# First strip of all 576 tokens of batch 0, second of 448, and batch 1's x by token

## The chip, the core and the metric

The kernel runs on one core of one Trainium2 chip. The metric is the device time of one execution in microseconds (us). The kernel before was timed three times: 312.16, 312.21 and 312.97, median 312.21. One further execution was profiled; it took 312.61, of which 310.8 is the span from the program's first to its last instruction.

## What is computed

Linear attention without softmax, a norm per head, and a bilinear feed-forward layer behind it. B=8 batches, H=8 heads, S=576 tokens, D=64; d_model=512, d_ff=1536; 4608 tokens in all.

```python
kv  = einsum('bhsd,bhse->bhde', k, v)
o   = einsum('bhsd,bhde->bhse', q, kv)
x   = o / sqrt(mean(o * o, axis=-1) + 1e-6) * g_norm
x   = x.transpose(0, 2, 1, 3).reshape(B * S, H * D)
out = ((x @ w_a) * (x @ w_b)) @ w_out
```

Inputs and output are fp32 in DRAM; the products run in bf16 and accumulate in fp32.

## The kernel before

**Tiling.** Heads go in pairs (NP=4), so that a pair fills 128 partitions. `xt` holds x with features on partitions and all 4608 tokens along the free side. The feed-forward layer works in 9 strips of 512 tokens (STRIP). A `Unit` is one of 12 blocks of d_ff (fc) of one strip: `part_a` makes four products (one per 128 features, kc) with `wa_t` into a PSUM bank and ScalarE copies it to `a_sb`; `part_b` does the same with `wb_t`, and VectorE multiplies bank and copy into `abt`. `ffn_ab` is one such unit with banks that rotate. After the 12 units the strip's output follows: `ffn_o` makes 12 products per group of 128 tokens, and `o_out` copies the bank to one of four `o_sb` and stores it from the SP queue.

**Two ways to x.** Batches 0 and 1 (EARLY) load q, k and v per pair with the cast to bf16 (`load_pair`). TensorE transposes q (`qtr`), makes kv (`kv1`), then x by feature: `px` for batch 0, `x` for batch 1 (with `kvb`, kv of two heads on the diagonal); ScalarE squares it (`psq`), TensorE sums the squares by a product with `ones` and ScalarE takes the root (`pss`), VectorE multiplies into `xt` (`pst`). Batches 2 to 7 make x by token: `load_late` copies q to a DRAM tile `qs` and loads k and v in another order, `transpose_q` brings q in transposed by a DMA from the SP queue; `tx` makes x of 128 tokens at a time (chunk c, five chunks of which the last has 64 tokens) in 40 small products; `tsq` squares (ScalarE), `tss` sums (VectorE), `trs` takes the root (ScalarE) and multiplies by g (GpSimd), `txt` multiplies (VectorE) and writes the chunk into `xt` by a DMA transpose from the SP queue.

**Order.** The order of every engine is written by hand (`manual_schedule`). The sequence is: batch 0's attention pair by pair; strip 0's units (from u0, line 539); then from line 567 strip 0's output groups, with batch 1's attention between their halves (`pieces`, lines 574 to 591); then strip 1's first two units (592 to 597); then the loop over strips from line 632, in which `slot(A, s, n)` places the by-token steps of batch s+1 between the units: in strip 1 kv of batch 2 stands at n=5 and `tx` at n=6.5. `halves` splits each product into two of 64 stationary columns.

**Queues.** The GpSimd (POOL) queue issues all loads with a cast, in this order: the rest of batch 0, the first 256 columns of wa and wb, the other five blocks of 256 columns, the twelve pieces of wo, batch 1's four pairs, `load_late(2)`. The SP queue issues stores and DMA transposes. Line 570 holds SP's queue until v of batch 1 has landed, before it loads `g_all`.

Of the kernel before, what the change touches and what calls it, by code (L numbers as in the profile page):

```python
# [9 lines left out]
BF16 = mybir.dt.bfloat16  # L10
# [5 lines left out]
def kernel(  # L16
# [26 lines left out]
    EARLY = 2  # L43
    KORD = tuple(range(KC))

    pool = ctx.enter_context(tc.tile_pool(name="sb", bufs=1))
    psum = ctx.enter_context(tc.tile_pool(name="ps", bufs=1, space=bass.MemoryType.PSUM))

    def sb(shape, dt, name):
        return pool.tile(shape, dt, name=name, tag=name)  # L50
# [15 lines left out]

    qT = [sb([128, NP, S], BF16, f"qT{i}") for i in range(2)]
    kvs = [sb([128, NP, D], BF16, f"kvs{i}") for i in range(2)]

    kvb = sb([128, NP, 128], BF16, "kvb")  # L70
    xt = sb([128, KC, n_tok], BF16, "xt")
    abt = [[sb([128, STRIP], BF16, f"ab{i}_{f}") for f in range(FC)] for i in range(2)]
    a_sb = [sb([128, STRIP], BF16, f"asb{i}") for i in range(4)]
    sq = [sb([128, 2, HF], BF16, f"sq{i}") for i in range(3)]
    rs = [sb([128, 2, HF], FP32, f"rs{i}") for i in range(3)]
# [53 lines left out]
    def load_ab(c0, c1):  # L129
        nc.gpsimd.dma_start(out=wa_t[:, :, c0:c1], in_=wa_v[:, :, c0:c1])  # L130
        nc.gpsimd.dma_start(out=wb_t[:, :, c0:c1], in_=wb_v[:, :, c0:c1])
# [27 lines left out]
    def product(o, lhsT, rhs, **kw):  # L159
        for r in (slice(0, D), slice(D, 2 * D)) if halves[0] else (slice(0, 2 * D),):  # L160
            nc.tensor.matmul(o[r], lhsT=lhsT[:, r], rhs=rhs, **kw)  # L161


    class Attn:
# [18 lines left out]
                        stop=(c == len(rows) - 1),  # L183
                    )

        def kv_out(self, ps, src):
            for j in range(2):
                r = slice(j * D, (j + 1) * D)
                nc.scalar.copy(kvb[r, ps, r], src[r])


        def kv1(self, p, i):
            self.kv(p, P[:, i, STRIP - D :])
# [56 lines left out]
                )  # L250


        def x(self, p, i0):
            for h in range(2):
                product(
                    P[:, i0 + h, 0:HF],
                    kvb[:, p, :],
                    self.qT[:, p, h * HF : (h + 1) * HF],
                    start=True,
                    stop=True,  # L260
                )

        def rows(self, c):
            t0 = min(c * 128, S - 128)
# [19 lines left out]
        def tx(self, lent):  # L286
            self.lent = lent
            for c in range(LC + 1):
                t0, _ = self.rows(c)
                for p in range(NP):  # L290
                    for j, (i, c0) in enumerate(self.place(c)):
                        r = slice(j * D, (j + 1) * D)
                        nc.tensor.matmul(  # L293
                            P[:, i, c0 + p * D : c0 + (p + 1) * D],
                            lhsT=self.qT[r, p, t0 : t0 + 128],
                            rhs=self.kvs[r, p, :],
                            start=True,
                            stop=True,
                        )


            _, r = self.rows(LC)
            for j, (i, _) in enumerate(self.place(LC)):
                nc.scalar.copy(
                    x_last[r, j], P[r, i, 0 : STRIP // 2].rearrange("t (p d) -> t p d", p=NP)
                )

        def tsq(self, c):
            _, r = self.rows(c)
# [7 lines left out]
                axis=mybir.AxisListType.X,  # L317
            )

        def trs(self, c):  # L320
            _, r = self.rows(c)
            n = r.stop - r.start
            nc.scalar.activation(  # L323
                rst[c % 3][r],
                sst[c % 3][r],
                AF.Abs_reciprocal_sqrt,
                bias=eps_t[r],
                scale=1.0 / D,
            )
            nc.gpsimd.tensor_mul(  # L330
                sqt[c % 3][r].rearrange("t j p d -> t (j p) d"),
                rst[c % 3][r].unsqueeze(2).to_broadcast([n, H, D]),
                g_all[r].unsqueeze(1).to_broadcast([n, H, D]),
            )
# [13 lines left out]
    class Unit:  # L348
        n = 0

        def __init__(self, s, fc, a, b):
            self.s, self.fc, self.a, self.b = s, fc, P[:, a, :], P[:, b, :]
            self.t = a_sb[Unit.n % 4]
            Unit.n += 1

        def mm(self, w, kcs):
            t0 = self.s * STRIP
            for kc in kcs:
                product(
                    self.a if w is wa_t else self.b,  # L360
                    w[:, kc, self.fc * 128 : (self.fc + 1) * 128],
                    xt[:, kc, t0 : t0 + STRIP],
                    start=(kc == KORD[0]),
                    stop=(kc == KORD[-1]),
                )
# [2 lines left out]
            self.mm(wa_t, kcs)  # L368
            self.mm(wb_t, kcs)

        def part_a(self, kcs=KORD):
            self.mm(wa_t, kcs)
            nc.scalar.copy(self.t, self.a)  # L373

        def part_b(self, kcs=KORD):
            self.mm(wb_t, kcs)
            nc.vector.tensor_mul(abt[self.s % 2][self.fc], self.b, self.t)  # L377

        def rest(self, kcs=KORD):
            self.part_a(kcs)  # L380
            self.part_b(kcs)

    ab_banks = [4, 1, 2, 0]

    def ab_bank():
        ab_banks.append(ab_banks.pop(0))
        return ab_banks[-1]

    def ffn_ab(s, fc, between=None):
        u = Unit(s, fc, ab_bank(), 0)  # L390
        u.part_a()
        if between:
            between()
        u.b = P[:, ab_bank(), :]
        u.part_b()

    def store(t0, t, e0, e1, eng=nc.sync):
# [14 lines left out]
    n_o = [0]  # L412

    def o_mm(s, g, i, fcs, e0=0, e1=d_model):
        for fc in fcs:
            product(
                P[:, i, e0:e1],
                abt[s % 2][fc][:, g * 128 : (g + 1) * 128],
                wo_t[:, fc, e0:e1],
                start=(fc == 0),  # L420
                stop=(fc == FC - 1),
            )
# [41 lines left out]
    make_identity(nc, ident, nomemset=True)  # L464
    nc.scalar.activation(warm, eps_t, AF.Abs_reciprocal_sqrt)
    nc.vector.memset(ones, 0.0)
    nc.vector.memset(kvb, 0.0)
    for t in ktl + vtl:
        nc.vector.memset(t[S - 128 * LC :, :, LC, :], 0.0)
    nc.vector.memset(ones[0:D, 0:D], 1.0 / D)  # L470
# [4 lines left out]
    for c in range(0, KC, 2):  # L475
        for w, src in ((wa_t, wa_v), (wb_t, wb_v)):
            nc.gpsimd.dma_start(out=w[:, c : c + 2, 0:WC], in_=src[:, c : c + 2, 0:WC])  # L477
    for i in range(1, d_ff // WC):
        load_ab(i * WC, (i + 1) * WC)
    for i in range(FC):  # L480
        load_o(i)
    for p in range(NP):
        load_pair(1, p)
    load_late(2)

    X, SS = (4, 0), 6

# [65 lines left out]
    u1.part_a((3,))  # L553
    u0.part_b((2, 3))
    u1.part_b((2, 3))

    u2 = Unit(0, 2, 0, 1)
    u3 = Unit(0, 3, 2, 0)
# [1 line left out]
    u3.part_a()  # L560
    u2.part_b()
    u3.part_b()
    for fc in range(4, FC):
        ffn_ab(0, fc)


    A = Attn(1)
    h1, h2 = range(0, FC // 2), range(FC // 2, FC)

    nc.sync.dma_start(out=gate_d, in_=vt[1][0:1, H - 1, EC - 1, D - 1 : D])  # L570
    nc.sync.dma_start(out=g_all, in_=g_norm.partition_broadcast(128))
    transpose_q(2)
    ffn_o(0, 0, X[0])
    pieces = [(1, h1), (1, h2), (2, h1), (2, h2), (3, h1), (3, h2)]
    for n, (g, fcs) in enumerate(pieces):

        halves[0] = n > 0
        o_mm(0, g, O, fcs)
        if fcs is h2:
            o_out(0, g, O)  # L580
        if 0 <= n - 2 < NP:
            A.pss(n - 2, SS)
            A.pst(n - 2, X[n % 2])
        if 0 <= n - 1 < NP:
            A.x(n - 1, X[(n - 1) % 2])
            A.psq(n - 1, X[(n - 1) % 2])
        if n < NP:
            A.qtr(n, 2)
            A.kv1(n, 2)
            A.kv_out(n, P[:, 2, STRIP - D :])  # L590
            A.qtr_out(n, 2)
    u0 = Unit(1, 0, 2, 3)
    u1 = Unit(1, 1, 4, 5)
    u0.first((0, 1, 2))
    u1.first((0, 1, 2))
    u0.rest((3,))
    u1.rest((3,))
    ab_banks[:] = [0, 1, 2]


    def slot(A, s, n):

        kb = P[:, 7, :].rearrange("q (b p e) -> q b p e", b=2, e=D)
        if s == 1:
            k0, xs = 5, (6.5, 8, 9.5, 11, 12.5)
        else:
            k0, x0 = {2: (2, 3.5), 3: (4, 5.5), 4: (0, 1.5), 5: (4, 5.5), 6: (0, 1.5)}[s]
            xs = tuple(x0 + x for x in (0, 1.5, 2.5, 4, 5))

        k0, x0 = {1: (5, 6.5), 2: (1, 2.5), 3: (4, 5.5), 4: (0, 0.5), 5: (4, 5.5), 6: (0, 0.5)}[s]  # L610
        if n == k0 and s in (1, 2, 3, 5):
            halves[0] = s < 5
            two = [A] if s < 3 else [A, Attn(s + 2)]
            for i, a in enumerate(two):
                for p in range(NP):
                    a.kv(p, kb[:, i, p, :])
            for i, a in enumerate(two):
                (nc.scalar.copy if i else nc.vector.tensor_copy)(a.kvs, kb[:, i])  # L618
        m = n - x0
        if m == 0:  # L620
            A.tx(ab_bank())
        for c in range(LC + 1):
            if m == 1.5 * c:
                A.tsq(c)
            if m == (1, 2, 4, 5, 7)[c]:
                A.tss(c)
            if m == (1, 2, 4, 5, 7)[c] + 0.5:
                A.trs(c)
            if m == (1, 2, 4, 5, 7)[c] + 1.5:
                A.txt(c)  # L630

    for s in range(1, N_STRIP - 1):
# [64 lines left out]
```

## Time and profile before

| What | Value |
|---|---|
| median of three runs | 312.21 us |
| profiled execution | 312.61 us |
| its span | 310.8 us |
| first feed-forward product | 14.10 us |
| strip 0's units end, first output group starts | 35.15 us |
| third unit of strip 1 starts | 53.41 us |
| strip 2 starts | 82.75 us |
| last weight block (wb) landed | 29.40 us |
| last load of batch 1 landed | 46.22 us |
| load_late(2): first issue, last landing | 41.34, 60.65 us |
| load_late(3): first issue, last landing | 62.39, 78.89 us |

The times of the lower rows are counted from the span's start and come from the timeline and from the issues with their landings. In lines of the profile, PE is TensorE, PEld its weight loads, DVE VectorE, ACT ScalarE, POOL GpSimd, SP the sync engine; `L161` is line 161 of the kernel. A form such as 128*64 128x512 is a product with 128 rows and 64 stationary columns that writes 512 columns. Lines of digits give the busy share of 40 equal slices of the span in tenths. "q0 software_dynamic" is the queue of DMAs issued by POOL, q1 that of SP; "share of 16 engines" can exceed 100% because packets overlap.

### The profile page before, as it was taken

The page shows a single profiled execution, that of the slowest core. Times are in us where ns is not written, and L with a number is a line of the kernel's source. Part 1 is how long each engine was busy: PE and PEld are TensorE (multiplying, and loading weights), DVE is VectorE, ACT ScalarE, POOL GpSimd, SP SyncE. Part 2 cuts the span into 40 slices and gives each one's busy share as a digit, 9 for nine tenths or more (in the row PEclk, how much of TensorE's full clock was granted, in tenths as well). Part 3 has the DMA queues.
Part 4 walks back from the last instruction along what each step waited for, and adds up shares of the span by engine and source line. Part 5 has one row for each costly group of instructions (what it writes and reads, how often), then busy time and mean ns, then how long its engine had stood idle before and what let it go on. Part 6 is the DMA issues. An engine that isn't in the chain of part 4 may idle for free.

```text
span 310.8 us, 6542 instructions
## 1 busy us (share of the span) xinstructions
PE 304.3 (98%) x2684; PEld 157.6 (51%) x2701; DVE 140.6 (45%) x235; ACT 117.0 (38%) x231; POOL 101.3 (33%) x123
## 2 busy tenths in 40 slices
PE   7899999999999999999999999999999999999996
PEld 3444476655555555555555555444444444444444
DVE  4544335458248603484386123752782143214321
ACT  3743255354255313551564034632651233123310
POOL 8954991093274630043646300221240000000000
PEclk9999999999999999999999999999999999999999
DMA  8999999999899999047998990073021200030002
GB/s 180 197 196 199 201 188 168 161 169 184 174 137 185 139 174 193 2 84 134 178 177 118 162 188 2 19 160 110 20 51 42 103 1 0 34 103 0 0 36 101
DMA packets 94403, 36.29 MB, mean 117 GB/s; under 512 B 64934, under 2 KB 89894, under 8 KB 94374
## 3 DMA queue, kind: packets, MB, share of 16 engines
q0 software_dynamic: 59120, 18.44, 56.6%
q1 hardware_dynamic: 34786, 16.93, 25.0%
q10 hardware_dynamic: 468, 0.51, 0.6%
q8 instruction: 21, 0.34, 0.5%
q14 instruction: 8, 0.07, 0.1%
HBM read 37.78 MB, written 12.98 MB: 163 GB/s over the span
## 4 chain that ended last, share of the span: by engine, by line
PE 79%; DMA 12%; POOL 7%; issue 1%; ACT 0%; POOLq 0%
PE P L161 77%; DMA wb_t<-in_moe_w_b_dram 6%; DMA vtl<-in_v_dram 4%; DMA wo_t<-in_moe_w_out_dram 2%; PE P L293 1%; PE P L178 1%; POOL vt L119 1%; POOL qt L119 1%; POOL qs L142 1%; POOL kt L119 1%; POOL wa_t L477 0%; POOL wb_t L477 0%; POOL wo_t L134 0%; POOL ktl L145 0%; POOL vtl L145 0%
## 5 line engine op out<-in xcount | busy, mean ns | idle before, releaser
L377 DVE TENSOR_TENSOR ab<-P,asb 128x512 bf16<-128x512 f32 x108 | 74.4, 691 | 103.2 <-PE P L161 99.9
L161 PE MATMUL P<-xt,wb_t 128*64 128x512 bf16 (+1 forms) x641 | 111.4, 379 | 0.2
L161 PE MATMUL P<-xt,wa_t 128*64 128x512 bf16 (+1 forms) x636 | 111.0, 379 | 0.6 <-issue 0.2
L373 ACT CAST asb<-P 128x512 bf16<-128x512 f32 x108 | 63.1, 586 | 89.6 <-PE P L161 89.5
L161 PE MATMUL P<-wo_t,ab 128*64 128x512 bf16 (+3 forms) x673 | 95.5, 371 | 0.3
L161 PEld LDWEIGHTS <-ab 128*64 128x64 bf16 (+1 forms) x678 | 47.5, 106 | 45.0
L161 PEld LDWEIGHTS <-wa_t 128*64 128x64 bf16 (+1 forms) x644 | 46.0, 106 | 46.2 <-issue 0.6
L161 PEld LDWEIGHTS <-wb_t 128*64 128x64 bf16 (+1 forms) x644 | 45.8, 106 | 45.8
L330 POOL TENSOR_TENSOR sqt<-rst,g_all 128x512 f32<-128x512 f32 (+1 forms) x24 | 25.0, 1046 | 83.0 <-ACT rst L323 83.0
L429 ACT COPY osb<-P 128x512 f32<-128x512 f32 x17 | 10.0, 586 | 70.2 <-PE P L161 60.2
L431 DVE COPY osb<-P 128x512 f32<-128x512 f32 x18 | 12.4, 691 | 44.9 <-PE P L161 40.4
L142 POOL DMA_DIRECT2D qs<-in_q_dram x12 | 19.8, 1654 | 0.7 <-issue 0.3
L314 DVE TENSOR_REDUCE sst<-sqt 128x8 f32<-128x512 f32 (+1 forms) x24 | 16.3, 680 | 1.7 <-ACT sqt L310 1.5
L339 DVE TENSOR_TENSOR qv<-P,sqt 128x512 bf16<-128x512 f32 x18 | 12.3, 681 | 0.0
L330 POOL TENSOR_TENSOR k_x<-rst,g_all 128x512 f32<-128x512 f32 x6 | 6.3, 1044 | 17.4 <-ACT rst L323 17.4
L323 ACT ACTIVATE rst<-sst,eps_t 128x8 f32<-128x8 f32 (+1 forms) x30 | 9.0, 300 | 7.2 <-DVE sst L314 7.0
L310 ACT ACTIVATE sqt<-P 128x512 f32<-128x512 f32 x18 | 10.5, 585 | 0.1
L243 DVE SCALAR_TENSOR_TENSOR xt<-P,g_col,rs 128x288 bf16<-128x288 f32 x16 | 7.5, 511 | 5.1 <-ACT rs L233 5.1
L134 POOL DMA_DIRECT2D wo_t<-in_moe_w_out_dram x12 | 6.4, 530 | 6.7 <-DMA wb_t<-in_moe_w_b_dram 3.2
L233 ACT ACTIVATE rs<-P,eps_t 128x576 f32<-128x576 f32 (+1 forms) x9 | 6.1, 689 | 3.7 <-PE P L161 3.4
L139 POOL COPY gate<-qT 1x1 bf16<-1x1 bf16 x5 | 0.9, 177 | 18.9 <-DVE kvs L618 14.0
L444 PE MATMUL P<-zeros 128*128 128x512 bf16 x16 | 5.8, 510 | 1.2 <-DVE eps_t L461 1.2
(72 smaller groups left out, 131.7 us busy)
## 6 DMA issues: line engine op xcount, KB each, us to landing
out_dram<-osb SPq DMA_DIRECT2D x23, 256.0 KB, 2.1
qs<-in_q_dram POOLq DMA_DIRECT2D x12, 288.0 KB, 7.5
ktl<-in_k_dram POOLq DMA_DIRECT2D x6, 512.0 KB, 9.6
vtl<-in_v_dram POOLq DMA_DIRECT2D x6, 512.0 KB, 12.2
out_dram<-osb SPq DMA_DIRECT2D x13, 128.0 KB, 2.4
wo_t<-in_moe_w_out_dram POOLq DMA_DIRECT2D x12, 128.0 KB, 6.0
wa_t<-in_moe_w_a_dram POOLq DMA_DIRECT2D x5, 256.0 KB, 8.9
wb_t<-in_moe_w_b_dram POOLq DMA_DIRECT2D x5, 256.0 KB, 9.5
```

What stands on the lines that cost most here:

```text
L119: nc.gpsimd.dma_start(out=t[:, hs, :, :], in_=src[b, hs].rearrange("h (t c) d -> t h c d", c=EC))
L142: nc.gpsimd.dma_start(out=d[:, hs, :], in_=q[b, hs].rearrange("h t d -> t h d"))
L161: nc.tensor.matmul(o[r], lhsT=lhsT[:, r], rhs=rhs, **kw)
L310: nc.scalar.activation(sqt[c % 3][r], self.by_head(c)[r], AF.Square)
L314: nc.vector.reduce_sum(sst[c % 3][r], sqt[c % 3][r].rearrange("t j p d -> t (j p) d"), axis=mybir.AxisListType.X,)
L323: nc.scalar.activation(rst[c % 3][r], sst[c % 3][r], AF.Abs_reciprocal_sqrt, bias=eps_t[r], scale=1.0 / D,)
L330: nc.gpsimd.tensor_mul(sqt[c % 3][r].rearrange("t j p d -> t (j p) d"), rst[c % 3][r].unsqueeze(2).to_broadcast([n, H, D]), g_all[r].unsqu ...
L339: nc.vector.tensor_mul(t[r].rearrange("t (p j) d -> t j p d", j=2), self.by_head(c)[r], sqt[c % 3][r])
L373: nc.scalar.copy(self.t, self.a)
L377: nc.vector.tensor_mul(abt[self.s % 2][self.fc], self.b, self.t)
L429: nc.scalar.copy(t, P[:, i, :])
L431: nc.vector.tensor_copy(t, P[:, i, :])
```

## The change

Strip 0 takes all 576 tokens of batch 0: its units are 448 columns wide (CUT), and after every second unit `ffn_end` makes the last 128 tokens of two fc blocks in one bank. Strip 1 takes the 448 tokens 576 to 1023. The twelve `abt` tiles hold both strips' columns side by side. Batch 1's x is made by token, as batches 2 to 7 make it: q's transposes and kv stand after fc 5, 8, 10 and 11 of strip 0, `tx` after the last unit, then the chain of squares, sums, roots and products, with two of the multiplications by g on VectorE instead of GpSimd. Batch 1's loads stand among the weight blocks and ahead of wo; `load_late(2)` stands behind the multiplications of chunks 0 and 1 on the GpSimd queue. Three output groups of strip 0 run side by side, block of wo by block of wo, then the fourth. Strip 1's first two units are made in pieces of 256 and 192 columns, and kv of batch 2 moves to n=7, its `tx` to n=8. SP's wait for v goes; SP waits for the second weight block instead. `x`, `kv_out` and `kvb` are removed.

```diff
+    CUT = S - 128
     pool = ctx.enter_context(tc.tile_pool(name="sb", bufs=1))
...
     kvs = [sb([128, NP, D], BF16, f"kvs{i}") for i in range(2)]
-    kvb = sb([128, NP, 128], BF16, "kvb")
     xt = sb([128, KC, n_tok], BF16, "xt")
-    abt = [[sb([128, STRIP], BF16, f"ab{i}_{f}") for f in range(FC)] for i in range(2)]
+    abt = [sb([128, 2 * STRIP], BF16, f"ab{f}") for f in range(FC)]
     a_sb = [sb([128, STRIP], BF16, f"asb{i}") for i in range(4)]
...
+        def last_out(self, j):
             _, r = self.rows(LC)
-            for j, (i, _) in enumerate(self.place(LC)):
-                nc.scalar.copy(
-                    x_last[r, j], P[r, i, 0 : STRIP // 2].rearrange("t (p d) -> t p d", p=NP)
-                )
+            i, _ = self.place(LC)[j]
+            nc.scalar.copy(
+                x_last[r, j], P[r, i, 0 : STRIP // 2].rearrange("t (p d) -> t p d", p=NP)
+            )
...
-        def trs(self, c):
+        def trs(self, c, eng=nc.gpsimd):
+            self.trsqrt(c)
+            self.tg(c, eng)
+        def trsqrt(self, c):
             _, r = self.rows(c)
-            n = r.stop - r.start
             nc.scalar.activation(
...
             )
-            nc.gpsimd.tensor_mul(
+        def tg(self, c, eng):
+            _, r = self.rows(c)
+            n = r.stop - r.start
+            eng.tensor_mul(
                 sqt[c % 3][r].rearrange("t j p d -> t (j p) d"),
...
         def __init__(self, s, fc, a, b):
-            self.s, self.fc, self.a, self.b = s, fc, P[:, a, :], P[:, b, :]
-            self.t = a_sb[Unit.n % 4]
+            self.t0, self.n, self.c0 = {0: (0, CUT, 0), 1: (S, 2 * STRIP - S, S)}.get(
+                s, (s * STRIP, STRIP, s % 2 * STRIP)
+            )
+            self.fc, self.a, self.b = fc, P[:, a, 0 : self.n], P[:, b, 0 : self.n]
+            self.t = a_sb[Unit.n % 4][:, 0 : self.n]
             Unit.n += 1
-        def mm(self, w, kcs):
-            t0 = self.s * STRIP
+        def mm(self, w, kcs, cols=None):
+            c0, c1 = cols or (0, self.n)
             for kc in kcs:
                 product(
-                    self.a if w is wa_t else self.b,
+                    (self.a if w is wa_t else self.b)[:, c0:c1],
                     w[:, kc, self.fc * 128 : (self.fc + 1) * 128],
-                    xt[:, kc, t0 : t0 + STRIP],
+                    xt[:, kc, self.t0 + c0 : self.t0 + c1],
                     start=(kc == KORD[0]),
...
-        def part_a(self, kcs=KORD):
-            self.mm(wa_t, kcs)
+        def part_a(self, kcs=KORD, cols=None):
+            self.mm(wa_t, kcs, cols)
             nc.scalar.copy(self.t, self.a)
-        def part_b(self, kcs=KORD):
-            self.mm(wb_t, kcs)
-            nc.vector.tensor_mul(abt[self.s % 2][self.fc], self.b, self.t)
-        def rest(self, kcs=KORD):
-            self.part_a(kcs)
-            self.part_b(kcs)
+        def part_b(self, kcs=KORD, cols=None):
+            self.mm(wb_t, kcs, cols)
+            nc.vector.tensor_mul(abt[self.fc][:, self.c0 : self.c0 + self.n], self.b, self.t)
+    def ffn_end(fc, i):
+        n = S - CUT
+        t = a_sb[Unit.n % 4][:, 0 : 2 * n]
+        Unit.n += 1
+        for m, w in enumerate((wa_t, wb_t)):
+            for j in range(2):
+                for kc in KORD:
+                    product(
+                        P[:, i, (2 * m + j) * n : (2 * m + j + 1) * n],
+                        w[:, kc, (fc + j) * 128 : (fc + j + 1) * 128],
+                        xt[:, kc, CUT:S],
+                        start=(kc == KORD[0]),
+                        stop=(kc == KORD[-1]),
+                    )
+        nc.scalar.copy(t, P[:, i, 0 : 2 * n])
+        for j in range(2):
+            nc.vector.tensor_mul(
+                abt[fc + j][:, CUT:S],
+                P[:, i, (2 + j) * n : (3 + j) * n],
+                t[:, j * n : (j + 1) * n],
+            )
...
     def o_mm(s, g, i, fcs, e0=0, e1=d_model):
+        c0 = s % 2 * STRIP + g * 128
         for fc in fcs:
...
                 P[:, i, e0:e1],
-                abt[s % 2][fc][:, g * 128 : (g + 1) * 128],
+                abt[fc][:, c0 : c0 + 128],
                 wo_t[:, fc, e0:e1],
...
             nc.gpsimd.dma_start(out=w[:, c : c + 2, 0:WC], in_=src[:, c : c + 2, 0:WC])
-    for i in range(1, d_ff // WC):
-        load_ab(i * WC, (i + 1) * WC)
+    load_ab(WC, 2 * WC)
+    load_ab(2 * WC, 3 * WC)
+    load_pair(1, 0)
+    load_ab(3 * WC, 4 * WC)
+    hs = [slice(2 * p, 2 * p + 2) for p in range(NP)]
+    load_heads(1, qt[1], q, hs[1])
+    load_heads(1, kt[1], k, hs[1])
+    load_ab(4 * WC, 5 * WC)
+    load_heads(1, vt[1], v, hs[1])
+    load_heads(1, qt[1], q, hs[2])
+    load_ab(5 * WC, 6 * WC)
+    load_heads(1, kt[1], k, hs[2])
+    load_heads(1, vt[1], v, hs[2])
+    load_pair(1, 3)
     for i in range(FC):
         load_o(i)
-    for p in range(NP):
-        load_pair(1, p)
-    load_late(2)
+    nc.sync.dma_start(out=gate_d, in_=wb_t[0:1, KC - 1, 2 * WC - 1 : 2 * WC])
+    nc.sync.dma_start(out=g_all, in_=g_norm.partition_broadcast(128))
...
     u1.part_b((2, 3))
+    ffn_end(0, 6)
...
     u3.part_b()
+    ffn_end(2, 7)
+    A = Attn(1)
+    def pair(p):
+        i = (3, 5)[p % 2]
+        A.qtr(p, i)
+        A.kv1(p, i)
+        A.kv1_out(p, i, nc.scalar.copy)
+        A.qtr_out(p, i)
     for fc in range(4, FC):
+        if fc == 9:
+            ab_banks.remove(4)
         ffn_ab(0, fc)
-    A = Attn(1)
-    h1, h2 = range(0, FC // 2), range(FC // 2, FC)
-    nc.sync.dma_start(out=gate_d, in_=vt[1][0:1, H - 1, EC - 1, D - 1 : D])
-    nc.sync.dma_start(out=g_all, in_=g_norm.partition_broadcast(128))
+        if fc in (5, 8, 10, 11):
+            halves[0] = True
+            pair((5, 8, 10, 11).index(fc))
+        if fc % 2:
+            ffn_end(fc - 1, (ab_banks[0] if fc == FC - 1 else 6 + fc // 2 % 2))
+    lent = ab_banks[1]
+    A.tx(lent)
+    A.last_out(0)
+    A.tsq(0)
+    A.last_out(1)
+    A.tsq(1)
+    A.tss(0)
+    A.trsqrt(0)
+    A.tg(0, nc.gpsimd)
+    A.tss(1)
+    A.trsqrt(1)
+    A.tg(1, nc.gpsimd)
+    A.tsq(2)
+    A.tss(2)
+    A.trsqrt(2)
+    A.txt(0)
+    A.tsq(3)
+    A.tg(2, nc.vector)
+    A.txt(1)
+    A.txt(2)
+    A.tss(3)
+    A.trsqrt(3)
+    A.tg(3, nc.vector)
+    A.txt(3)
+    A.tsq(4)
+    A.tss(4)
+    A.trsqrt(4)
+    load_late(2)
+    A.tg(4, nc.gpsimd)
     transpose_q(2)
-    ffn_o(0, 0, X[0])
-    pieces = [(1, h1), (1, h2), (2, h1), (2, h2), (3, h1), (3, h2)]
-    for n, (g, fcs) in enumerate(pieces):
-        halves[0] = n > 0
-        o_mm(0, g, O, fcs)
-        if fcs is h2:
-            o_out(0, g, O)
-        if 0 <= n - 2 < NP:
-            A.pss(n - 2, SS)
-            A.pst(n - 2, X[n % 2])
-        if 0 <= n - 1 < NP:
-            A.x(n - 1, X[(n - 1) % 2])
-            A.psq(n - 1, X[(n - 1) % 2])
-        if n < NP:
-            A.qtr(n, 2)
-            A.kv1(n, 2)
-            A.kv_out(n, P[:, 2, STRIP - D :])
-            A.qtr_out(n, 2)
-    u0 = Unit(1, 0, 2, 3)
-    u1 = Unit(1, 1, 4, 5)
-    u0.first((0, 1, 2))
-    u1.first((0, 1, 2))
-    u0.rest((3,))
-    u1.rest((3,))
+    three = (ab_banks[2], ab_banks[0], ab_banks[1])
+    for fc in range(FC + 2):
+        for g, i in enumerate(three):
+            f = fc - (0, 0, 2)[g]
+            if 0 <= f < FC:
+                o_mm(0, g, i, (f,))
+                if f == FC - 1:
+                    o_out(0, g, i)
+    ffn_o(0, 3)
+    u0 = Unit(1, 0, 4, 5)
+    u1 = Unit(1, 1, 6, 7)
+    c = 256
+    for u in (u0, u1):
+        u.mm(wa_t, KORD, (0, c))
+        u.mm(wb_t, KORD, (0, c))
+    for u in (u0, u1):
+        u.part_a(KORD, (c, u.n))
+        u.part_b(KORD, (c, u.n))
+    A.txt(4)
     ab_banks[:] = [0, 1, 2]
...
         kb = P[:, 7, :].rearrange("q (b p e) -> q b p e", b=2, e=D)
-        if s == 1:
-            k0, xs = 5, (6.5, 8, 9.5, 11, 12.5)
-        else:
-            k0, x0 = {2: (2, 3.5), 3: (4, 5.5), 4: (0, 1.5), 5: (4, 5.5), 6: (0, 1.5)}[s]
-            xs = tuple(x0 + x for x in (0, 1.5, 2.5, 4, 5))
-        k0, x0 = {1: (5, 6.5), 2: (1, 2.5), 3: (4, 5.5), 4: (0, 0.5), 5: (4, 5.5), 6: (0, 0.5)}[s]
+        k0, x0 = {1: (7, 8), 2: (1, 2.5), 3: (4, 5.5), 4: (0, 0.5), 5: (4, 5.5), 6: (0, 0.5)}[s]
         if n == k0 and s in (1, 2, 3, 5):
...
             A.tx(ab_bank())
+            A.last_out(0)
+            A.last_out(1)
+        sums = (1, 2, 4, 5, 6 if s == 1 else 7)
         for c in range(LC + 1):
-            if m == 1.5 * c:
+            if m == (5 if s == 1 and c == LC else 1.5 * c):
                 A.tsq(c)
-            if m == (1, 2, 4, 5, 7)[c]:
+            if m == sums[c]:
                 A.tss(c)
-            if m == (1, 2, 4, 5, 7)[c] + 0.5:
+            if m == sums[c] + 0.5:
                 A.trs(c)
-            if m == (1, 2, 4, 5, 7)[c] + 1.5:
+            if m == sums[c] + (1 if s == 1 and c == LC else 1.5):
                 A.txt(c)
     for s in range(1, N_STRIP - 1):
```

## The prediction

> **What bounds the kernel now.** I read the page's head first.
>
> ```profile
> PE 304.3 (98%) x2684; PEld 157.6 (51%) x2701; DVE 140.6 (45%) x235; ACT 117.0 (38%) x231; POOL 101.3 (33%) x123
> DMA  8999999999899999047998990073021200030002
> ```
>
> TensorE is busy 98% of a 310.8 us span, while the DMA engines are full for the first 130 us or so. A change pays only if TensorE's queue gets shorter or loses a wait, and the early part is where a transfer can make it wait. The TensorE timeline of the stretch that is rewritten comes second; a column gives the start, so two starts give the true pitch (the second column overlaps its neighbour).
>
> ```profile
> 21.34 1.03 PE L161 MATMUL P<-xt,wa_t 128*128 128x512 bf16 x4
> 22.20 1.03 PE L161 MATMUL P<-xt,wb_t 128*128 128x512 bf16 x4
> ...
> 39.13 0.45 PE L202 MATMUL P<-ident,qt 96*64 96x96 bf16 x12
> 39.60 0.38 PE L178 MATMUL P<-vt,kt 96*64 96x64 bf16 x12
> ...
> 43.31 0.44 PE L161 MATMUL P<-sq,ones 128*64 128x288 bf16 x4
> 43.55 0.44 PE L161 MATMUL P<-qT,kvb 128*64 128x288 bf16 x4
> 43.80 0.45 PE L202 MATMUL P<-ident,qt 96*64 96x96 bf16 x12
> 44.05 0.38 PE L178 MATMUL P<-vt,kt 96*64 96x64 bf16 x12
> ```
>
> Four products of 512 columns take 22.20-21.34 = 0.863 us, 0.216 each. Batch 1's x and its sum of squares take 0.245 us per pair each; its transposes take 0.25 when data is there, but 0.47 at 39.13, because vt of pair 0 lands at 39.56. So TensorE waits for batch 1's loads there; the same at 41.33 (0.49).
>
> Third, the narrow products at the kernel's end, by source line:
>
> ```profile
> L161 PE MATMUL P<-wo_t,ab x26: 219/219/273, 306.1 to 307.6; 128*128 128x128 bf16 x24, 128*128 128x256 bf16 x2
> ```
>
> Read singly, starts step by 0.109 us at 256 columns and 0.056 at 128. So a product costs its columns at 0.417 ns each plus about 2.5 ns, and 448 columns cost 0.189.
>
> **The change on TensorE, part by part.** The times are those of the profiled execution (312.61 us, that is 1.8 around the span).
> - Strip 0 narrowed to 448 columns: the first two units gain little, because they wait for xt of pair 3 (DVE L243, 15.60 to 16.54) either way; six products follow it, 6 x 0.027 = -0.16. The other 80: 80 x 0.027 = -2.13.
> - ffn_end: six calls of 16 products of 128 columns, 96 x 0.056 = +5.36.
> - Strip 1: 80 products at 448, -2.13; its first two units in pieces of 256 and 192 columns, 16 x (0.109 + 0.082) against 16 x 0.216, -0.38.
> - Gone: x and pss of batch 1, eight groups at 0.245, -1.96. Added: one tx, 0.69 us as the chain of waits has each of the others (L293 x40). qtr and kv move, 0.44 per pair, no cost.
> - Waits gone: vt twice, 0.22 + 0.24; 0.13 at 45.54 (0.38 instead of 0.25); batch 2's kv at 60.32, which holds 0.87 us for 0.63 of work because vtl lands at 60.65, and which moves from n=5 to n=7: 0.24. Together -0.83.
> - A small new wait: the second output group uses the bank of the last ffn_end, freed only by its ACT copy (about 0.37) and two DVE products (0.29 each by width from the 0.69 of L377). About +0.3.
>
> Sum: -0.16-2.13+5.36-2.13-0.38-1.96+0.69-0.83+0.3 = **-1.24 us**.
>
> **Do the loads come in time?** No load is added ahead of load_late(2); 35 moved or old ones precede wo. A POOL issue starts 0.28 us after the landing of the one eight before it (16.59 after 16.31, 18.98 after 18.70), and pieces land every 1.34 us (256 KB), 0.74 (144 KB) and 0.65 (128 KB). Adding these in the new order from 18.70, weight block 5 lands by 34.6, pair 3 at 36.8, 37.6, 38.3, and wo from 39.0 to 46.1. TensorE, added up as above, wants block 5's wb at about 36, pair 3's v at 38.9, wo's first at 40.7 and, taken chunk by chunk by three groups, the last at 47.5. Slacks are 0.5 to 1.7 us. The cover is thin, but the price of a 5% slower stream (1.2 us late) is under 0.8.
>
> **The step that decides: x of batch 1 by DMA transpose.** tx ends near 41.0. Until strip 1 there are 48 output products, 10.4 us, so its first columns (chunks 0, 1) are wanted at 51.3, chunks 2 and 3 at 53.1, 16 x 0.109 later. The chain by rows of the last batch (start to start): copy 0.33, square 0.60, sum 0.72, root 0.40, tensor_mul on POOL 1.05 (on DVE about 0.65), product 0.71 to SP's issue; DVE holds them in the order written. That gives SP's issues at 45.7, 46.9, 48.1 and 50.0. What is queued behind: SP carries transpose_q(2) and the stores, which nobody wants before 60; POOL carries load_late(2) behind chunk 1's tensor_mul, so its first qs issue moves from 41.34 to about 45.2, **just among the transposes**. All ten transposes after 199 us, with no load running, took:
>
> ```profile
> DMA to landing us min/median/max: 2.3/2.4/2.5
> ```
>
> At 2.4, the four land by 49.3 and 52.4, in time. With a load running, the next two answers are the transpose issued at 147.49 (1.8 us behind a qs issue) and the two at 70.61 and 72.26 (8 behind it):
>
> ```profile
> DMA to landing us min/median/max: 5.2/5.2/5.2
> ...
> DMA to landing us min/median/max: 6.8/7.0/7.2
> ```
>
> One at 168.22, 1.0 behind, took 4.6. From 70.6 to 74.5 the only queue with packets is the load's, though a transpose was issued at 70.61:
>
> ```profile
> q0 software_dynamic: 1867, 0.74, 155.2%
> issues: line engine op xcount, KB each, median us to landing
> xt<-qv SPq DMA_TRANSPOSE x2, 7.0
> ```
>
> The Trainium skill (DMA: Bandwidth & Descriptors, Queues, rings and completion order) says that each DMA engine takes turns between the queues that have work, packet by packet. By it a 0.13 MB transpose beside a load would need perhaps 1 us more than alone, 3.4 as an estimate, the last chunk would be 0.3 late, and the sum would stay near -1. This trace shows 4.6 to 7.2, so the rows decide.
>
> Bounds of the wait: none at 2.4. At 4.6 each, chunk 1 lands at 51.5 (0.2 late) and chunk 3 at 54.6 against 53.3 (1.3): 1.5. At 7.2 each, 2.8 and then 1.3: 4.1. I take the nearest row for each: chunk 1 follows the qs issue by 1.7 us, so 5.2, landing 52.1, 0.8 late; chunk 3 follows by 4.8, between the rows at 1.8 and 8, so 6.2, landing 56.2 against 53.9, 2.3 late. Together **+3.1**. Batch 2's own load starts later too, but load_late(3)'s pattern (16.5 us from first issue, 62.39, to last landing, 78.89) puts vtl at 61.7 and kv's n=7 at about 67, so nothing waits there.
>
> -1.24 + 3.1 = +1.9: 314.5 on the profiled run's own count, which lies 0.4 above the median shown (312.21). So **314.1 us**.
>
> **Rivals.**
> - All hidden: transposes land in 2.4 to 3, as with an idle queue, since the last wo bytes leave at 46.1 and a qs issue moves its first bytes only some 2.5 us later. Then -1.24, 311.0 us, and faster. It decides from the point where chunk 1 lands before 51.3 and chunk 3 before 53.1. For: the first transpose surely slips through. Against: three of the four come after the qs issue, and none of the rows so placed is under 4.6. A limit on it: batch 2's third transpose, issued at 77.11 for a strip at 82.75, would come under load_late(3) pushed back about a microsecond while strip 2 starts earlier; up to 0.8 of the gain could go there. Chance 0.31.
> - Lightly delayed, 3.5 to 4.6: a wait of 0.5 to 1.7, so -0.7 to +0.5, 311.5 to 312.7, mostly no change. Chance 0.14.
> - Heavily delayed: 7 us each, or the loads in strip 0 late too (0.8): +2.9 to +3.7, 315.1 to 315.9. Chance 0.10.
> - The forecast, waits of 2 to 4: chance 0.45.
>
> No row shows TensorE idle long enough to lose its clock (granted 1.00 throughout). The Trainium skill (TensorE: Matmul & The Clock Gate, The HAM clock gate) says about 3.4 us of idleness halves it; two waits of 0.8 and 2.3 would stay below, and by the rule alone a longer one could add up to 1.7.
>
> **Range and chances.** 310.6 to 315.9: from all hidden with 0.4 to spare, to the heavy case. The likeliest case's own range is 313 to 315. About 0.3% (0.9 us) can be told from no change here. Faster 0.32, same 0.12, slower 0.56.
>
> **What would show it.** Right: TensorE idle in front of strip 1's first units (two gaps, 0.8 and some 2), ended by transposes into xt landing 4.6 us or more after SP's issue; products in strip 0 at 0.189 and 0.056; no wait for vt or wo; kv of batch 2 without a gap. Wrong: transposes at 2.4 beside the qs packets; or a TensorE gap in strip 0 or among the output groups, so that the loads decide; or strip 2 waiting for batch 2, which I count as free.

## The result and the profile after

The changed kernel takes 324.54 us (median of four, 323.95 to 327.65) against 312.28 before: 4.1% slower, ratio 1.0408 with a 95% interval of 1.034 to 1.0476. The forecast had the sign and the first mechanism, but about a seventh of the size: +1.8 us was foretold, +12.3 came. The profiled execution is the longest of the four (327.65; span 325.8, 15.0 more than before); its mean granted clock is 0.984, that of the other three 0.988 to 0.989.

The page's head of the changed kernel:

```profile
PE 309.0 (95%) x2953; PEld 164.0 (50%) x2967; DVE 146.3 (45%) x250; ACT 117.5 (36%) x237; POOL 104.5 (32%) x126
PEclk9999999799995999999999999999999999999999
DMA  8999989999999529904799994045211200021002
```

TensorE's share falls from 98% to 95%, and the granted clock has two dents that the kernel before does not have. The TensorE timeline of the changed kernel, with the length of each idle stretch and what ended it in brackets:

```profile
22.56 0.92 PE L162 MATMUL P<-xt,wa_t 128*128 128x448 bf16 x4
23.31 0.92 PE L162 MATMUL P<-xt,wb_t 128*128 128x448 bf16 x4
...
41.08 10.70 PE L162 MATMUL P<-wo_t,ab 128*64 128x512 bf16 x96
54.20 0.63 PE L162 MATMUL P<-xt,wa_t 128*64 128x256 bf16 x8 [2.42 <-DMA xt<-qv]
...
58.93 0.52 PE L162 MATMUL P<-xt,wa_t 128*64 128x192 bf16 x8 [2.80 <-DMA xt<-qv]
...
91.30 1.05 PE L162 MATMUL P<-xt,wa_t 128*64 128x512 bf16 x8 [2.23 <-DMA xt<-qv]
...
98.83 1.92 PE L162 MATMUL P<-xt,wa_t 128*64 128x512 bf16 x8 [3.26 <-DVE ab L374]
```

Strip 0 runs as reckoned: four products of 448 columns in 0.75 us, and the output groups start at 41.08 where I had about 41. Then there are four waits: two in front of and between strip 1's first products, one in front of strip 2, one in strip 2. The first two are for batch 1's transposes, whose landing in this kernel was (transposes into xt issued from 46 to 51 us):

```profile
DMA to landing us min/median/max: 4.3/6.8/8.4
```

One by one they took 4.27, 6.58, 7.07 and 8.37, where 2.4 would have been in time and I had taken 5.2 for the second and 6.2 for the fourth. In the four later traces with the load in the same place the fourth took 8.8 to 9.0. The clock in the stretches 60.27 to 64.23 and 91.3 to 104.0 (columns: length, busy of PE, PEld, DVE, ACT, POOL, granted clock, DMA share, GB/s):

```profile
60.27:64.23 3.96, 3.96 (x31) 1.99 (x26) 2.35 (x4) 0.95 (x2) 0.00 (x0) 0.57 1.40 191
91.30:104.00 12.70, 9.44 (x96) 5.44 (x95) 3.00 (x5) 1.75 (x3) 5.96 (x7) 0.76 1.62 181
```

With each pair of waits came a stretch at half clock: 3.41 us long from 60.28, behind the second wait, and 6.83 from 97.82, within the fourth. The third and fourth wait come from queue orders, shown by the timelines of SP, then of POOL and VectorE, of the changed kernel:

```profile
84.23 3.16 SPq L155 DMA_TRANSPOSE qT<-qs  x1
87.49 1.00 SPq L425 DMA_DIRECT2D out_dram<-osb  x2
88.58 1.24 SPq L336 DMA_TRANSPOSE xt<-qv  x1
```

```profile
89.51 0.18 POOL L140 COPY gate<-qT 1x1 bf16<-1x1 bf16 x1 [2.84 <-DMA qT<-qs]
89.76 3.31 POOL L143 DMA_DIRECT2D qs<-in_q_dram  x2
...
96.30 1.03 POOL L323 TENSOR_TENSOR sqt<-rst,g_all 64x512 f32<-64x512 f32 x1
```

```profile
97.36 0.69 DVE L332 TENSOR_TENSOR qv<-rs,sqt 64x512 bf16<-64x512 f32 x1 [8.72 <-POOL sqt L323]
98.08 1.29 DVE L374 TENSOR_TENSOR ab<-P,asb 128x512 bf16<-128x512 f32 x2
```

SP issues the transpose of batch 2's chunk 2 (88.58), which strip 2 needs, behind transpose_q(3) and two stores. POOL does chunk 4's multiplication (96.30) behind the whole of load_late(4), whose gate waits for qT of batch 3; VectorE stands 8.72 us at chunk 4's product, the units' products queue behind it, and TensorE finds no free bank.

The account of the profiled runs, from starts of products; where a wait begins, its start is reckoned from the last start and the products' pitch. The two waits for batch 1's x +5.8 (54.20 less 51.44, 58.93 less 55.94); the first half clock +1.7 (half of 3.41); the wait for chunk 2 +2.4 (91.30 less 88.90); TensorE's own work and small waits -1.3 (strip 2 starts at 91.30 against 82.75, less these three terms; 0.2 of it is an earlier first product); VectorE's wait +3.45; the second half clock while products ran +2.9 (half of 104.65 less 98.83). Sum +14.9; measured +15.0.

### The profile page after: what moved, and what is told of

Its sections match the earlier page's. It is cut to its first block, busy times and chain, and to the rows that moved or that the text cites. A ratio compares the mean times of both kernels' runs of the same rounds, so it can differ in the third digit from the quotient of the medians.

```text
span 325.8 us, 7120 instructions
## 1 busy us (share of the span) xinstructions
PE 309.0 (95%) x2953; PEld 164.0 (50%) x2967; DVE 146.3 (45%) x250; ACT 117.5 (36%) x237; POOL 104.5 (32%) x126
## 4 chain that ended last, share of the span: by engine, by line
PE 86%; DMA 6%; ACT 2%; DVE 2%; POOL 2%; issue 2%; ACTq 0%; DVEq 0%; POOLq 0%
PE P L162 81%; DMA xt<-qv 3%; DMA qT<-qs 2%; PE P L278 2%; DMA qv<-in_v_dram 2%; PE P L179 1%; PE P L198 1%; DVE qv L332 1%; ACT sqt L296 1%; PE P L212 0%; POOL qs L143 0%; DVE sst L300 0%; ACT sq L221 0%; POOL sqt L323 0%; DVE xt L239 0%
## 5 line engine op out<-in xcount | busy, mean ns | idle before, releaser
L162 PE MATMUL P<-xt,wa_t 128*64 128x512 bf16 (+7 forms) x758 | 115.2, 360 | 11.2 <-DMA xt<-qv 7.4
L374 DVE TENSOR_TENSOR ab<-P,asb 128x512 bf16<-128x512 f32 (+1 forms) x108 | 72.9, 676 | 107.0 <-PE P L162 94.7
L162 PE MATMUL P<-xt,wb_t 128*64 128x512 bf16 (+7 forms) x761 | 114.2, 357 | 0.2
L370 ACT CAST asb<-P 128x512 bf16<-128x512 f32 (+1 forms) x108 | 61.8, 573 | 97.4 <-PE P L162 97.1
L162 PEld LDWEIGHTS <-wa_t 128*64 128x64 bf16 (+1 forms) x764 | 50.2, 109 | 55.8 <-issue 11.6
L162 PEld LDWEIGHTS <-wb_t 128*64 128x64 bf16 (+1 forms) x764 | 50.2, 108 | 43.9 <-issue 1.6
L323 POOL TENSOR_TENSOR sqt<-rst,g_all 128x512 f32<-128x512 f32 (+1 forms) x27 | 28.0, 1039 | 95.6 <-ACT rst L312 95.5
L300 DVE TENSOR_REDUCE sst<-sqt 128x8 f32<-128x512 f32 (+1 forms) x28 | 19.1, 681 | 3.5 <-ACT sqt L296 3.3
L296 ACT ACTIVATE sqt<-P 128x512 f32<-128x512 f32 x21 | 12.3, 586 | 0.5 <-DVE qv L332 0.3
L332 DVE TENSOR_TENSOR qv<-rs,sqt 64x512 bf16<-64x512 f32 x7 | 4.8, 690 | 8.9 <-POOL sqt L323 8.7
L278 PEld LDWEIGHTS <-qT 64*128 64x128 bf16 x280 | 4.7, 97 | 2.9 <-issue 2.8
```

What stands on the lines that cost most here:

```text
L278: nc.tensor.matmul(P[:, i, c0 + p * D : c0 + (p + 1) * D], lhsT=self.qT[r, p, t0 : t0 + 128], rhs=self.kvs[r, p, :], start=True, stop=True,)
L296: nc.scalar.activation(sqt[c % 3][r], self.by_head(c)[r], AF.Square)
L300: nc.vector.reduce_sum(sst[c % 3][r], sqt[c % 3][r].rearrange("t j p d -> t (j p) d"), axis=mybir.AxisListType.X,)
L323: eng.tensor_mul(sqt[c % 3][r].rearrange("t j p d -> t (j p) d"), rst[c % 3][r].unsqueeze(2).to_broadcast([n, H, D]), g_all[r].unsqueeze(1 ...
L332: nc.vector.tensor_mul(t[r].rearrange("t (p j) d -> t j p d", j=2), self.by_head(c)[r], sqt[c % 3][r])
L374: nc.vector.tensor_mul(abt[self.fc][:, self.c0 : self.c0 + self.n], self.b, self.t)
```

## The experiments

The late waits come first, since they were not foretold, with the cause of the early ones beside them; then what can be won back; then the split by itself. The kernel before took 312.46 to 312.47 beside them (medians).

**One place on GpSimd's queue.**

```diff
-            if b + 2 < B and n == (14, 10, 14, 8)[s - 1]:
+            if b + 2 < B and n == (15, 10, 14, 8)[s - 1]:
                 load_late(b + 2)
```

> The changed kernel with load_late(4) one place later in strip 1 (n=15), so that GpSimd's multiplication for batch 2's chunk 4 stands ahead of it in the queue. Theory: the 3.3 us in which TensorE waits for VectorE near 95.6 us of the changed kernel come from this order alone (GpSimd is held by the load's gate and its issues, VectorE stands at txt(4) behind it, and units' products queue behind VectorE). Then that wait goes, and with it the second stretch at half clock (6.8 us): 318 to 321 us. Rival, the loads of batches 2 and 3 are simply late: the same wait reappears at another instruction within some us and the time stays at 323 or more.

320.16 us (319.1 to 321.11), ratio 1.0244 (1.0218 to 1.0269), as expected. The wait at VectorE and the second half clock are gone; in front of strip 2 a wait of 1.35 us stays:

```profile
89.76 1.05 PE L162 MATMUL P<-xt,wa_t 128*64 128x512 bf16 x8 [1.35 <-DMA xt<-qv]
```

So one place of one call was worth 4.4 us, and the theory holds.

**One place on SP's queue.**

```diff
-            if b + 1 < B and n == (12, 4, 8, 5, 8)[s - 1]:
+            if b + 1 < B and n == (14, 4, 8, 5, 8)[s - 1]:
                 transpose_q(b + 1)
```

> The changed kernel with transpose_q(3) moved from n=12 to n=14 of strip 1, so that the DMA transpose of batch 2's chunk 2 stands ahead of it on the SP queue. Theory: the 2.2 us wait in front of strip 2 goes, but qT of batch 3 lands some 2 us later, the gate of load_late(4) with it, and the wait at VectorE near 95.6 us grows by as much: 322.5 to 325 us in all. Rival, chunk 2 is late because its chain or the load beside it is slow, not because of SP's order: the wait in front of strip 2 stays at 2 us or more.

330.08 us (329.12 to 332.95), ratio 1.0592 (1.0537 to 1.0647). The wait in front of strip 2 is gone, as expected; but the time lies 5 us above the expectation, because the other wait grew by nearly 6 us, not 2. GpSimd and TensorE in the timeline of this run:

```profile
91.68 0.18 POOL L140 COPY gate<-qT 1x1 bf16<-1x1 bf16 x1 [6.27 <-DMA qT<-qs]
...
98.46 1.04 POOL L323 TENSOR_TENSOR sqt<-rst,g_all 64x512 f32<-64x512 f32 x1
...
101.00 1.92 PE L162 MATMUL P<-xt,wa_t 128*64 128x512 bf16 x8 [9.11 <-DVE ab L374]
```

The gate opens 2.2 us later, and strip 2 starts at 87.64 instead of 91.30, so the block on GpSimd is met 3.7 us sooner: 2.4 of that is the wait that strip 2 lost, the rest lies in front of it (in this trace the first half clock fell between the two early waits). A wait removed in front of a fixed obstacle only lengthens the wait at it. The clock adds a longer half (10.24 us from 95.11).

**Both.** The two edits together.

> Both edits together: load_late(4) at n=15 and transpose_q(3) at n=14 of strip 1. Theory: no wait of a microsecond or more after strip 1's first units, one stretch at half clock (the first) left: 315.5 to 318.5 us. What is left over the kernel before is then the wait for batch 1's transposes, some 5.8 us, with 1.7 us of half clock, less 1.2 saved. Rival, late loads: a wait of 2 us or more remains in strip 2.

318.91 us (317.74 to 319.53), ratio 1.02 (1.0177 to 1.0223), 0.4 above the range expected. After strip 1's first units no wait of 0.2 us is left. GpSimd now does chunk 4's multiplication ahead of the gate:

```profile
88.93 1.04 POOL L323 TENSOR_TENSOR sqt<-rst,g_all 64x512 f32<-64x512 f32 x1 [1.72 <-ACT rst L312]
93.31 0.18 POOL L140 COPY gate<-qT 1x1 bf16<-1x1 bf16 x1 [3.34 <-DMA qT<-qs]
```

The remaining 6.4 us over the kernel before lies where I had foretold a wait, in front of and between strip 1's first products, with one half clock behind it:

```profile
54.60 0.63 PE L162 MATMUL P<-xt,wa_t 128*64 128x256 bf16 x8 [2.70 <-DMA xt<-qv]
...
59.48 0.52 PE L162 MATMUL P<-xt,wa_t 128*64 128x192 bf16 x8 [2.94 <-DMA xt<-qv]
```

**The load out of the transposes' way.**

```diff
-    load_late(2)
     A.tg(4, nc.gpsimd)
+    load_late(2)
```

> The changed kernel with load_late(2) behind chunk 4's multiplication on GpSimd, so that its first packets flow after batch 1's transposes are issued. Theory, the transposes are slow because the load runs beside them: the four land 2.3 to 3.5 us after their issue, the two waits in front of strip 1's first units fall from 2.4 and 2.8 us to under 0.5 each, the first stretch at half clock goes; but k and v of batch 2 land near 69 us and kv at n=7 waits some 5 us for them. Time 320 to 326 us, for the later waits remain. Rival, a transpose in this place is slow by itself (four in a row on one queue, or wo's loads): the waits in front of strip 1 stay above 2 us.

326.64 us (326.11 to 327.05), ratio 1.0451 (1.0436 to 1.0467), 0.6 above the range expected. The four transposes into xt in this run, and the TensorE timeline behind them:

```profile
DMA to landing us min/median/max: 2.4/2.4/2.5
```

```profile
51.74 0.60 PE L162 MATMUL P<-xt,wa_t 128*64 128x256 bf16 x8
...
68.65 0.42 PE L179 MATMUL P<-vtl,ktl 128*64 128x64 bf16 x8 [4.59 <-DMA vtl<-in_v_dram]
69.95 1.06 PE L179 MATMUL P<-vtl,ktl 128*64 128x64 bf16 x32 [0.88 <-DMA vtl<-in_v_dram]
```

The same transposes in the same place on the same queue take 2.4 us when the load's packets come later, and strip 1 starts without a wait: the load beside them is the cause, not four in a row by themselves. But the load then ends at 69.91, and kv of batch 2 waits for it: the wait has moved. (The late waits of the changed kernel are in this run too, 3.90 us in front of strip 2 and 1.70 at VectorE; the order edits are not.) Its third unit of strip 1 starts 40.60 us after the first feed-forward product, against 39.31 before; less the 2.13 that strip 1's narrower units save later, that is -0.84 for the work on TensorE, where the prediction's terms without batch 2's kv give -1.0.

**The load in between,** with both order edits.

```diff
-    A.tg(3, nc.vector)
+    A.tg(3, nc.gpsimd)
+    load_late(2)
...
-    load_late(2)
-    A.tg(4, nc.gpsimd)
+    A.tg(4, nc.vector)
```

> Both order edits of strip 1, and load_late(2) behind chunk 3's multiplication, which goes back to GpSimd, while chunk 4's goes to VectorE: the load's first packets then come some 2.5 us after about 50.4 us, when all four transposes of batch 1 have been issued. Theory: the transposes land in 2.4 to 3.5 us and the waits in front of strip 1 fall under 0.5 us, but the load ends about 3 us later than in the changed kernel, near 67 us, and kv at n=7, due near 63.8, waits 3 to 4 us for it. 314 to 317.5 us: better than the two order edits alone (318.9), not better than the kernel before. Rival, the wait is only the load's place and costs nothing when it is moved: 311 to 312.5 us.

317.41 us (317.28 to 317.83), ratio 1.0159 (1.0144 to 1.0175): the best of the versions with batch 1's x by token, and still 1.6% slower than the kernel before. The first three transposes, then the fourth, issued some 0.6 us behind the load's first issue:

```profile
DMA to landing us min/median/max: 2.4/2.4/2.5
...
DMA to landing us min/median/max: 4.8/4.8/4.8
```

The time stands where expected, but the waits do not. In front of strip 1 under 0.5 us was expected, and the fourth transpose costs 2.32; for kv 3 to 4 was expected, and it waits 0.80; 1.44 lie in front of strip 2. By the trace batch 2's transposes run beside load_late(3) there (one took 6.9 us); no run tests that.

**Keeping TensorE busy,** with both order edits.

```diff
     c = 256
+    dummy(10, 7)
     for u in (u0, u1):
         u.mm(wa_t, KORD, (0, c))
         u.mm(wb_t, KORD, (0, c))
+    dummy(11, 2)
```

> Both order edits of strip 1, and products on zeros in the two waits: ten of 512 columns in front of strip 1's first products, eleven between their first and second pieces. Nothing else moves. Theory: TensorE is kept busy through the waits, so the clock is never granted at half and the 1.7 us that the 3.4 us at half clock cost go; the transposes still end the waits at the same time: 316.5 to 317.8 us against 318.9. Rival, the half clock costs nothing beside the waits: 318.5 to 319.5.

318.40 us (317.44 to 319.11), ratio 1.0187 (1.0164 to 1.0209): above the 316.5 to 317.8 expected and just under the rival's 318.5 to 319.5. The four times overlap with those of the two edits alone (median 318.91). Windows of this run:

```profile
51.50:60.00 8.50, 7.62 (x73) 4.33 (x73) 0.93 (x2) 1.24 (x3) 1.37 (x2) 1.00 1.73 162
60.00:64.00 4.00, 4.00 (x58) 2.63 (x54) 2.68 (x5) 1.93 (x4) 0.00 (x0) 1.00 1.42 181
```

The clock stays at 1.00 (0.57 from 60 to 64 in the run without the dummy products), and it does so in all four executions; the four without dummy products have 0.989 to 0.995 in the mean. In the two traces the sixteen pieces of 192 columns and the eight products of 448 behind them take 2.85 us instead of 4.53, so the half clock's 1.7 us is there to be had; in the medians 0.5 shows, less than the runs scatter. What the half clock costs a typical execution stays open.

**The split alone.** The kernel before with CUT, the single set of ab tiles, `ffn_end` and units of 448 columns; all else as before.

```diff
+    ffn_end(2, 7)
     for fc in range(4, FC):
         ffn_ab(0, fc)
+        if fc % 2:
+            ffn_end(fc - 1, 6 + fc // 2 % 2)
```

> The kernel before with the split alone: strip 0 of 576 tokens by ffn_end, strip 1 of 448, one set of ab tiles; batch 1's x stays by feature, the loads and the groups' order stay. Theory: the split costs TensorE about +0.5 us (96 products at 0.056 against 26.7 ns saved on 176 others, and ten more at the start that wait anyway); strip 0's units end 3 us later, so the two waits for vt (0.46) and batch 2's kv wait (0.24) go: 311.7 to 312.7 us, within 0.3% of the kernel before. Rival, narrow products cost more than their columns (weight loads show): 314 or more.

312.83 us (ten runs, 312.6 to 313.43), ratio 1.0014 (1.0004 to 1.0023): within 0.3% and 0.1 above the range expected. The narrow products cost no more than their columns: strip 0's units from the first `ffn_end` to the first output group take 20.50 us, and 80 x 0.189 + 96 x 0.056 gives the same:

```profile
17.93 0.61 PE L162 MATMUL P<-xt,wa_t 128*128 128x128 bf16 x8
...
38.43 4.05 PE L162 MATMUL P<-wo_t,ab 128*128 128x512 bf16 x18
```

The split by itself is no gain, and of the 12 us it explains 0.4.

## Why the prediction was wrong, point by point

- **TensorE's own work.** Right: -0.84 measured up to strip 1's third unit against -1.0 without kv, and -1.3 up to strip 2 against -1.24; the narrow products, the moved loads and the vt waits came as reckoned. The loads landed within about a microsecond of the sum (pair 3's v at 39.14 against 38.3, wo's last at 46.93 against 46.1) and cost 0.13.
- **"The step that decides".** The mechanism was right and is shown by the load's move: 4.3 to 8.4 us beside the load, 2.4 without it. The size failed: 5.8 us, not 3.1. The last transpose alone settles the sum: 2.2 of the missing 2.7 are its landing (8.37, not 6.2), 0.5 its issue (50.52, not 50.0). The upper bound of 4.1, at 7.2 each, was itself too low. I took for each transpose the row with the nearest distance to a load's first issue, but the rows of 4.6 and 5.2 were single transposes, and here four stand in a row beside one load. Whether their company or the later stretch of the load made them longer, no run separates. The distance was a poor guide in the trace before too: it has two, issued at 101.31 and 102.86 beside the end of a load, at 3.9 and 2.9, which the rows of 4.6 to 7.2 leave out; and the 2.4 of the ten without a load rests on the six whose landing the profile has.
- **"So nothing waits there".** This is the step that failed most. I followed batch 2 to kv and tx and not through the queues that its chunks are moved past. With tx at n=8 instead of 6.5, chunk 2's transpose falls from n=12 to n=13.5, behind transpose_q(3) at n=12, and chunk 4's multiplication from n=14 to n=14.5, behind load_late(4) at n=14. The two places and the clock behind them are worth 324.54 - 318.91 = 5.6 us, shown by the paired edit. Even without them the time lies 3.0 above the range, by the early waits and their half clock. The rival "all hidden" even named a late third transpose, but put it down to the load, at most 0.8.
- **"Two waits of 0.8 and 2.3 would stay below".** They were 2.8 and 3.0 with products between them, and the clock halved: in the profiled execution +1.7, and +2.9 at the late waits, where the sum had nothing.
- **The range.** It held the early wait's bounds and no price for the late ones; 324.54 lies 8.6 above its end.

What no run here settles: whether a plan with later kv for batch 2, and every later load moved to match, could beat 312.3. The most that TensorE's terms leave is about 1 us, an estimate from the prediction's sum; it was not tried.

## What to carry to other kernels

When a step moves by a place or two in an order written by hand, list for every queue (SP's and GpSimd's too) what it now stands behind, and follow each of its pieces to its deadline; here nearly half of a 12 us loss came from two calls that stood still while other work was moved behind them. A DMA transpose that lands in 2.4 us with no load running took over 8 beside one, so a schedule is made with the loaded time, and for several in a row not with one alone. Taking away one wait in front of a blocked engine can make the whole slower (330.08 against 324.54 here), so such order edits are also tested together.

## What the hardware showed that was not expected

The clock did not need an idle stretch of 3.4 us. Five traces show half clock amid the kernel, those of the changed kernel and of the first four experiments. In them its stretches begin and end on a grid of 3.41 us, and each of the eight began after a grid window in which TensorE was busy 39% or less (39, 34, 29, 29, 27, 27, 13 and 6); windows at 43, 50, 51, 53 and 57%, and one at 56% in the run with the load in between, began none. Two windows of the changed kernel (columns: length, busy of PE, granted clock, DMA share, GB/s), the first with half clock behind it, the second without:

```profile
56.86:60.28 3.42, 1.35 (x34) 1.00 1.54 186
87.58:91.00 3.42, 1.48 (x14) 1.00 0.93 217
```

A window at half clock with TensorE 70% busy did not end it, one with 97% did. The Trainium skill (TensorE: Matmul & The Clock Gate, The HAM clock gate) gives the same window of about 3.4 us, free-running, but speaks of an idle one; in these runs a mostly idle one was enough.

What such a stretch costs depends on where it falls. In the trace of the one edit on GpSimd's queue it lay on the products between the two early waits (from 54.84); they took 3.2 us instead of 1.7, and the wait behind them was 1.81 instead of 2.80, so part of the loss was hidden.
